# A linear-attention block with a gated feed-forward: the attention matrix M made in three fp32r passes, its late operands loaded elsewhere, and the instruction order given as a list of due times

## The chip, the cores and the metric

The kernel runs on one core of a Trainium2 chip. A core has a matrix engine (TensorE, PE in the profile, with PEld for its weight loads), a vector engine (VectorE, DVE), an activation engine (ScalarE, ACT), a general engine (GpSimd, POOL) and a queue engine (SyncE, SP) that here issues every DMA. Matrix products land in PSUM, which has eight banks of 128 x 512 fp32; other tiles lie in SBUF, in 128 partitions. The metric is the device time of one execution in microseconds; lower is better.

## The reference, cut to what matters

```python
def _A_ref(x, wqkv, wo):                 # x: 1 x 2048 x 512, 32 heads of 16
    q, k, v = split(x @ wqkv)
    phi = lambda t: where(t > 0, t + 1, exp(t)) + 1e-6
    pq, pk = phi(q), phi(k)
    kv = einsum("bhsd,bhse->bhde", pk, v)
    z = einsum("bhsd->bhd", pk)
    num = einsum("bhqd,bhde->bhqe", pq, kv)
    den = einsum("bhqd,bhd->bhq", pq, z)[..., None] + 1e-6
    return merge_heads(num / den) @ wo

def _B_ref(x, w_gate, w_up, w_down):     # 512 -> 1792 -> 512
    return (gelu(x @ w_gate) * (x @ w_up)) @ w_down

xn = layernorm(x)
return x + _A_ref(xn, wqkv, wo) * silu(_B_ref(xn, w_gate, w_up, w_down))
```

## The kernel before, in words

**Arithmetic.** All large products run in fp32r, the matrix engine's reduced fp32, in three passes: an operand is split into a high part (an ACT copy that rounds to fp32r) and a low part (the subtraction of the high part, on DVE or now and then on POOL), and high x high, high x low and low x high are added up in PSUM (`split`, line 640; `Sum`, line 646; `three`, line 671). Products of weights with 256 or 512 columns are further cut by a Strassen scheme of seven products in place of eight (`PRODUCTS`, line 212). A few small products were left in fp32.

**Stages.** In the first 135 us or so the tokens are normalised and turned, k and q are made from them, phi is taken, and `gps` gathers the sum over tokens of phi(k) times the normalised x (line 956). So v is never made: `GT` (four tiles, copied from `gps` after line 1140) times the v weights gives the k-v sums `pkv` of all heads (line 1203), which a mask cuts to the heads' own blocks, `kv4` (line 1205). `zacc` gathers phi(k) itself on POOL; a product with a matrix of ones, `pz` (line 1148), adds it up over the partitions for the denominator. Then the attention matrix M = kv4 x wo is made in four products, `pm` (lines 1207 to 1214), split into high and low, and stored to HBM as `m_d`. The attention's output is later one product `S` of M with the scaled phi(q) features (`sps`, in `attn`, line 1463), for four chunks of 512 tokens in the order 2, 3, 0, 1.

The feed-forward runs in two passes over the same 14 weight tiles, seven pairs of gate and up (`ffn`, line 1398). The first pass (`p` = 1) handles chunks 2 and 3 while the weights are split and stored to HBM as `w_d`; the second (`p` = 0) handles chunks 0 and 1 with the weights loaded back. `F` products (`fprod`, PSUM names FX, FY, FZ) make gate and up, `E` products (`down_strassen`, names dX, dY, dZ) go down to `acc`. The S products of chunk 2 stand between the E products at the end of the first pass, those of chunk 3 at the end of the second, and those of chunks 0 and 1 after everything.

**Places.** SBUF is cut by hand into pools of numbered places: `xf` holds the x forms in a high and a low place; `wp` three weight places used in a ring and a fourth for sums; `rawp` three places (R0, R1, TMP) for raw gate and up weights, which only the first pass reads; `dp` a draw place and four that hold accumulators in a pass; `up` 36 places of 128 x 512. A new tile in a place waits for all work on the tile before it. `load_m` (line 1451) loads M's two halves of 1 MB into the weight ring: at the end of the second pass they take the places of the last but two and the last but one weight tile. The features of chunk 3, eight pieces of 256 KB (high and low, loaded as such), then go to the low x place, those of chunk 0 to the high one, and those of chunk 1 to the low one again.

**Order.** Every instruction is recorded by `do` (line 270) with an engine, a cost in us and its tiles. `order` (line 309) decides the order on all engines ahead of time, from a list of PE keys written out by hand (`pe_keys`) and a due time `late` for each operation. `forward` (line 440) plays the program through with the recorded costs: at each step an engine takes, among its ready operations, the one with the least `late`; PE may run ahead of its list by 6 us (`AHEAD`, line 262). Before, eight passes of `latest` and `forward` found the due times, and 216 draws (`KEPT`, line 19) then altered some of them, each by at most 4 us for chosen operations (`altered`, line 332). The engines run the result in that order on the chip; a wait that comes out longer than the planner thought holds its whole engine.

Around the change, the hand-written list has the z product after five F products of the first pass, the k-v sums after twelve, and the four M products three F products later. M product number 0 to 3 use PSUM banks 6, 7, 5 and 6.

Of the kernel before, what the change touches and what calls it, by code (L numbers as in the profile page):

```python
# [15 lines left out]
P = 128  # L16
EPS_LN = 1e-5
EPS = 1e-6
KEPT = [
    (55, 70, [720000004]),  # L20
    (115, 135, [720000005]),
    (200, 270, [720000009]),
    (500, 560, [720000027]),
    (-1, 12, [720000035]),
    (70, 85, [720000040]),
    (-1, 12, [720000043]),
    (25, 40, [720000085, 720000134]),
    (200, 270, [720000140]),
    (-1, 12, [720000144]),
    (200, 270, [720000152]),  # L30
    (340, 420, [720000172, 720000184]),
    (100, 115, [720000203]),
    (340, 420, [720000233]),
    (500, 560, [720000243]),
    (40, 55, [720000247]),
    (560, 605, [720000257]),
    (200, 270, [720000279]),
    (340, 420, [720000290]),
    (500, 560, [720000362]),
    (200, 270, [720000390]),  # L40
    (55, 70, [720000517]),
    (40, 55, [720000540]),
    (340, 420, [720000555]),
    (270, 340, [720000602, 720000649, 720000655]),
    (340, 420, [720000658]),
    (270, 340, [720000690]),
    (500, 560, [720000887]),
    (12, 25, [720000899]),
    (55, 70, [720000957]),
    (500, 560, [720000974]),  # L50
    (40, 55, [720001218]),
    (-1, 12, [720001311]),
    (25, 40, [720001456]),
    (115, 135, [720001543]),
    (40, 55, [720001818]),
    (25, 40, [720001887]),
    (85, 100, [720001895]),
    (135, 200, [720001949]),
    (340, 420, [720002052]),
    (500, 560, [720002094]),  # L60
    (115, 135, [720002310]),
    (100, 115, [720002326]),
    (500, 560, [720002367]),
    (135, 200, [720002396]),
    (40, 55, [720002422]),
    (270, 340, [720002472]),
    (200, 270, [720002488]),
    (55, 70, [720002565, 720002605]),
    (115, 135, [720002669]),
    (100, 115, [720002694]),  # L70
    (55, 70, [720002734]),
    (40, 55, [720002796]),
    (100, 115, [720002858]),
    (40, 55, [720002901]),
    (340, 420, [720002982]),
    (70, 85, [720003200]),
    (420, 500, [720003430]),
    (-1, 12, [720003440]),
    (40, 55, [720003709, 720003813]),
    (70, 85, [720003981]),  # L80
    (115, 135, [720004064]),
    (25, 40, [720004170]),
    (100, 115, [720004402]),
    (500, 560, [720004624, 720004745]),
    (420, 500, [720004920]),
    (340, 420, [720005018]),
    (420, 500, [720005191]),
    (500, 560, [720005291]),
    (340, 420, [720005364]),
    (270, 340, [720005386]),  # L90
    (500, 560, [720005573]),
    (270, 340, [720005617]),
    (500, 560, [720005700, 720005753, 720005812]),
    (70, 85, [720005857]),
    (100, 115, [720005876, 720006137]),
    (200, 270, [720006523]),
    (340, 420, [720006542]),
    (270, 340, [720006565]),
    (500, 560, [720006740]),
    (270, 340, [720006762]),  # L100
    (420, 500, [720006797]),
    (100, 115, [720006937]),
    (25, 40, [720007069]),
    (100, 115, [720007820]),
    (270, 340, [720007916]),
    (200, 270, [720007997]),
    (100, 115, [720008028]),
    (40, 55, [720008434]),
    (70, 85, [720008559]),
    (40, 55, [720008706]),  # L110
    (55, 70, [720008751]),
    (-1, 12, [720008785, 720010301]),
    (25, 40, [720011151]),
    (-1, 12, [720011236]),
    (500, 560, [720011560]),
    (340, 420, [720011716]),
    (270, 340, [720011832]),
    (55, 70, [720011869, 720011995]),
    (40, 55, [720012578, 720013114]),
    (135, 200, [720013435]),  # L120
    (12, 25, [720013929]),
    (270, 340, [720014337]),
    (70, 85, [720015269]),
    (340, 420, [720015275]),
    (12, 25, [720015459]),
    (340, 420, [720016007]),
    (55, 70, [720016730]),
    (100, 115, [720016972]),
    (40, 55, [720017118]),
    (420, 500, [720019299, 720019742]),  # L130
    (25, 40, [720023341]),
    (560, 605, [720025689]),
    (200, 270, [720026707, 720027204]),
    (500, 560, [720027907]),
    (200, 270, [720029093]),
    (270, 340, [720029251]),
    (200, 270, [720030011]),
    (135, 200, [720030869]),
    (500, 560, [720031562]),
    (25, 40, [720032237]),  # L140
    (70, 85, [720033404]),
    (500, 560, [720034357]),
    (70, 85, [720034379]),
    (55, 70, [720034598]),
    (135, 200, [720037606]),
    (70, 85, [720037790, 720038397]),
    (200, 270, [720038864, 720039585]),
    (270, 340, [720041466]),
    (340, 420, [720041524]),
    (270, 340, [720041782]),  # L150
    (340, 420, [720043687]),
    (270, 340, [720043952]),
    (500, 560, [720044378]),
# [1492 lines left out]
```

## Time and profile before

| | us |
|---|---|
| median of 3 runs | 602.98 |
| lowest, highest | 602.73, 603.38 |
| the profiled execution | 602.79 |
| its span, first to last instruction | 601.1 |
| PE busy in the span | 593.4 |
| DVE busy | 499.3 |
| ACT busy | 367.4 |
| POOL busy | 242.0 |

The profile is one execution. Rows of the timeline give the start, the length, the engine, the line, the operation, the tile that is written, an arrow, the tiles that are read, and how many alike stand in a row; in square brackets stands how long the engine was idle before, and what released it. PE instructions overlap in the pipeline, so a single pass of 0.39 us in the rows occupies less than that of PE's time: the step from start to start is the measure. Nearly all products have the line of one helper (665), copies 632 and subtractions 638, so the tile names tell them apart. Rows "SPq" are the queue engine issuing DMAs.

### The profile page before, as it was taken

How to read it: one execution, taken by the hardware profiler on the slowest of the kernel's cores; microseconds unless marked ns; L12 is line 12 of the kernel's file. 1: busy time of each engine (PE TensorE's matmuls, PEld its weight loads, DVE VectorE, ACT ScalarE, POOL GpSimd, SP SyncE). 2: the span in 40 equal slices, each digit the busy share in tenths (PEclk: the TensorE clock that was granted, in tenths of full speed). 3: DMA queues.
4: the chain of work that ended last, by engine and by line, in shares of the span. 5: the costliest groups of instructions: out<-in, count | busy, mean ns of one | idle time of the engine just before them, and what ended most of it. 6: DMA issues, size and time to landing. Idle time of an engine off the chain costs nothing.

```text
span 601.1 us, 7826 instructions
## 1 busy us (share of the span) xinstructions
PE 593.4 (99%) x2626; PEld 481.2 (80%) x2626; DVE 499.3 (83%) x768; ACT 367.4 (61%) x663; POOL 242.0 (40%) x237
## 2 busy tenths in 40 slices
PE   8999999999999999999999999999999999999997
PEld 6887788777878888888887788888888888887786
DVE  6999988988788989999877675757698889898887
ACT  6687778877677765655545469567454544545620
POOL 4455856847636763605043730521122221206000
PEclk9999999999999999999999999999999999999999
DMA  7149977758986245467975899944656566648967
GB/s 271 46 131 281 287 229 237 235 186 275 379 314 226 91 158 209 158 210 299 336 231 184 323 393 381 332 163 140 210 174 210 175 228 201 218 156 269 364 219 269
DMA packets 78807, 141.27 MB, mean 235 GB/s; under 512 B 4656, under 2 KB 47664, under 8 KB 74672
## 3 DMA queue, kind: packets, MB, share of 16 engines
q1 hardware_dynamic: 78768, 140.79, 67.9%
q8 instruction: 20, 0.33, 0.2%
q14 instruction: 19, 0.16, 0.1%
HBM read 87.82 MB, written 52.95 MB: 234 GB/s over the span
## 4 chain that ended last, share of the span: by engine, by line
PE 85%; DVE 6%; DMA 6%; issue 1%; ACT 1%; SPq 0%; ACTq 0%; DVEq 0%
PE FX L665 25%; PE FZ L665 13%; PE dX L665 12%; PE FY L665 6%; PE gps L665 6%; PE dY L665 6%; PE X L665 4%; PE dZ L665 3%; DMA g<-g_d 2%; PE Z L665 2%; PE q L665 2%; PE sps L665 2%; PE k L665 2%; DMA pqh<-t_d 1%; PE Y L665 1%
## 5 line engine op out<-in xcount | busy, mean ns | idle before, releaser
L665 PE MATMUL FX<-Xh,w 128*128 128x512 f32 x448 | 134.7, 391 | 0.0
L1374 POOL TENSOR_TENSOR h<-h,g 128x512 f32<-128x512 f32 x28 | 38.9, 1390 | 150.5 <-DVE h L638 150.2
L665 PEld LDWEIGHTS FX<-Xh,w 128*128 128x128 f32 x448 | 83.9, 188 | 18.2 <-ACT fu L632 0.4
L665 PE MATMUL FX<-Xl,w 128*128 128x512 f32 x224 | 68.8, 389 | 0.0
L665 PE MATMUL FZ<-Xh,w 128*128 128x512 f32 x224 | 68.3, 391 | 0.0
L632 ACT COPY fu<-FX 128x512 f32<-128x512 f32 x56 | 32.9, 587 | 45.7 <-PE FX L665 43.2
L632 ACT COPY dY<-dX 128x512 f32<-128x512 f32 x56 | 32.0, 571 | 40.0 <-DVE acc L1328 30.6
L632 ACT CAST hfh<-sums 128x512 fp32r<-128x512 f32 x56 | 34.7, 622 | 27.9 <-DVE sums L638 27.7
L665 PEld LDWEIGHTS FZ<-Xh,w 128*128 128x128 f32 x224 | 42.0, 188 | 9.2 <-issue 0.5
L665 PEld LDWEIGHTS FX<-Xl,w 128*128 128x128 f32 x224 | 42.0, 188 | 8.8
L665 PE MATMUL dX<-hfh,dh 128*128 128x512 f32 x112 | 43.8, 395 | 0.3 <-ACT dY L632 0.3
L665 PE MATMUL dX<-hfl,dh 128*128 128x512 f32 x112 | 43.6, 391 | 0.0
L638 POOL TENSOR_TENSOR tmp<-raw 128x256 f32<-128x256 f32 x28 | 24.6, 886 | 47.2 <-ACT fu L632 24.1
L665 PE MATMUL dX<-hfh,dl 128*128 128x512 f32 x112 | 43.5, 390 | 0.0
L1328 DVE TENSOR_TENSOR acc<-acc,dX 128x512 f32<-128x512 f32 x48 | 32.9, 685 | 11.3 <-PE dX L665 10.7
L638 DVE TENSOR_TENSOR hfl<-sums,hfh 128x512 fp32r<-128x512 f32 x56 | 39.9, 721 | 2.5 <-ACT hfh L632 1.7
L1328 DVE TENSOR_TENSOR acc<-acc,dY 128x512 f32<-128x512 f32 x48 | 32.8, 684 | 10.8 <-PE dY L665 10.6
L638 POOL TENSOR_TENSOR sums<-draw 128x256 f32<-128x256 f32 x28 | 23.5, 850 | 34.9 <-DMA draw<-in_B_w_down 26.1
L638 DVE TENSOR_TENSOR hfl<-h,hfh 128x512 fp32r<-128x512 f32 x42 | 34.1, 817 | 1.6 <-ACT hfh L632 1.6
L638 DVE TENSOR_TENSOR h<-fu,FZ 128x512 f32<-128x512 f32 x28 | 19.2, 687 | 18.4 <-ACT fu L632 13.3
L665 PE MATMUL FY<-Xh,w 128*128 128x512 f32 x112 | 34.5, 390 | 0.0
L665 PE MATMUL FZ<-Xl,w 128*128 128x512 f32 x112 | 34.3, 389 | 0.0
(205 smaller groups left out, 1513.5 us busy)
## 6 DMA issues: line engine op xcount, KB each, us to landing
w<-w_d SPq DMA_DIRECT2D x17, 1792.0 KB, 7.9
w_d<-w SPq DMA_DIRECT2D x11, 1792.0 KB, 8.1
draw<-in_B_w_down SPq DMA_DIRECT2D x14, 512.0 KB, 6.4
w_d<-we SPq DMA_DIRECT2D x18, 256.0 KB, 2.1
x<-in_A_x SPq DMA_DIRECT2D x16, 256.0 KB, 4.5
q_d<-qp SPq DMA_DIRECT2D x16, 256.0 KB, 3.0
qz<-q_d SPq DMA_DIRECT2D x16, 256.0 KB, 3.7
q<-q_d SPq DMA_DIRECT2D x16, 256.0 KB, 3.9
```

Of the source, the lines that this page charges most:

```text
L632: do("ACT", act(n, src.psum), lambda o, i: nc.scalar.copy(o, i), dst, src, name=name)
L638: do(eng, c, lambda o, p, q: getattr(e, f"tensor_{op}")(o, p, q), dst, a, b, name=name)
L665: nc.tensor.matmul(o if r is None else o[:, r], a, b, start=first, stop=made == self.passes[r], skip_group_check=self.on or r is not None)
L1328: do("DVE", dve(D), lambda o, i: nc.vector.tensor_add(o, o, i), o, ps, name="acc")
L1374: do("POOL", pool(NC), lambda o, i: nc.gpsimd.tensor_mul(o, o, i), h, g, name="h")
```

## The change

1. The z product: `zacc` and the matrix of ones become fp32r tiles (ones by a copy, zacc by a split into two), and two fp32r passes replace the fp32 product.
2. M: `kv4` and the four wo tiles are split into high and low, and each M product becomes three fp32r passes. The wo pieces lie in the four `dp` places that the accumulators use later. In the hand-written list the M products come six F products after the k-v sums, not three.
3. At the end of the second pass M is loaded by a new function: its high half in two pieces to the raw places R0 and R1, its low half to one place of the weight ring. Chunk 3's features go to the next place of the weight ring (seven pieces) and to the raw place TMP (one). Chunk 0 then takes the low x place and chunk 1 the high one. The first pass's end still uses `load_m`.
4. The due times: `KEPT`, the draws and the passes of `latest` are gone; a list `LATE` of 3626 numbers in hundredths of a us, one for each operation in the order of recording, sets `late`, and one `forward` pass makes the order.

```diff
-KEPT = [
-    (55, 70, [720000004]),
...
-]
+LATE = [
+    -69366, -1060, -1881, 3921, -71310, -201580, -181669, -555, -187235, 1065, -80, 116, -316, 1915, 1687, 2067, 1147, 1663, -377, -1166, -3532,
...
+    58321, 58073, 58004, -53919, -56946, -43454,
 ]
...
-        best = None
-        done = self.ops_in_turn(pe)
-
-        for n in range(8):
-            self.latest(done, now, capacity=n > 0)
-            done = self.forward(pe)
-            end = max(t for t, _ in done)
-            if best is None or end < best[0]:
-                best = end, done, {o: o.late for o in self.ops}
-
-
-        for lo, hi, draws in KEPT:
-            for n in draws:
-                best = self.altered(n, lo, hi, pe, *best)
-        return [o for _, o in best[1]]
...
+        for o, late in zip(self.ops, LATE, strict=True):
+            o.late, o.lat0 = late / 100, o.lat
+        return [o for _, o in self.forward(pe)]
...
     pz = bank(7, "pz")
-    do("PE", 0.9, lambda o, a, b: nc.tensor.matmul(o, a, b, start=True, stop=True), pz, ones, zacc, key="z")
+    ones_r = tile_in("sm", "onr", [P, P], F32R, "ones_r")
+    do("ACT", 0.2, lambda o, i: nc.scalar.copy(o, i), ones_r, ones, name="ones")
+    zs = [tile_in("up", n, [P, D], F32R, f"z{n}") for n in (29, 32)]
+    split(*zs, zacc, D, "z")
+
+    def run_z(o, a, *zs):
+        for n, z in enumerate(zs):
+            nc.tensor.matmul(o, a, z, start=n == 0, stop=n == 1)
+    do("PE", 2 * PASS, run_z, pz, ones_r, *zs, key="z")
...
+    kvs = [tile_in("up", n, [P, KT, P], F32R, f"kv{n}") for n in (23, 33)]
+    split(*kvs, kv4, D, "kv")
+    wos = []
+    for g in range(KT):
+        v = tile_in("dp", 1 + g, [P, 2, D], F32R, f"wos{g}", 2)
+        wos.append([v.part(v.res[hl:hl + 1], (slice(None), hl)) for hl in range(2)])
+        split(*wos[g], wo_sb[g], D, "wo")
     for g in range(KT):
         pm = bank([6, 7, 5, 6][g], f"pm{g}")
-        do("PE", 0.9, lambda o, a, b, g=g: nc.tensor.matmul(o, a[:, g, :], b, start=True, stop=True),
-           pm, kv4, wo_sb[g], key=("m", g))
+        Sum(pm).add(("m", g), *three([[v[:, g] for v in kvs]], [wos[g]]), name="m")
...
+    def load_m_early():
+
+        high = [tile_in("rawp", r, [P, 2, D], F32R, f"Mh{r}") for r in (R0, R1)]
+        for r, m in enumerate(high):
+            src = View([m_d(k, ()).res[0] for k in (2 * r, 2 * r + 1)], m_d(0, (0, slice(None), slice(2 * r, 2 * r + 2))).get)
+            dma(m.map(lambda ap: ap.bitcast(F32)), src, 512)
+        low = tile_in("wp", ring("w", [0, 1, 2]), [P, KT, D], F32R, "Ml")
+        src = View([m_d(KT + k, ()).res[0] for k in range(KT)], m_d(KT, 1).get)
+        dma(low.map(lambda ap: ap.bitcast(F32)), src, 1024)
+        return [lambda k, rows: high[k // 2][:, k % 2, rows], lambda k, rows: low[:, k, rows]]
...
-    pe_keys += keys[2:5] + ["z"] + keys[5:KV] + [("kv", g) for g in range(KT)] + keys[KV:KV + 3]
-    pe_keys += [("m", g) for g in range(KT)] + keys[KV + 3:]
+    pe_keys += keys[2:5] + ["z"] + keys[5:KV] + [("kv", g) for g in range(KT)] + keys[KV:KV + 6]
+    pe_keys += [("m", g) for g in range(KT)] + keys[KV + 6:]
...
-    M = load_m()
+    M = load_m_early()
+    pq = [tile_in("wp", ring("w", [0, 1, 2]), [P, 7, D], F32R, "pqw", 7), tile_in("rawp", TMP, [P, 2, D], F32R, "pqt", 1)]
     vs = {hl: tile_in("xf", hl, [P, 14, NC], F32R, f"pq{hl}", 14) for hl in "lh"}
...
-    for c, hl in zip(CHUNKS[1:], "lhl"):
+    attn(CHUNKS[1], M, lambda i, n: pq[(i - KT) // 7].part(
+        pq[(i - KT) // 7].res[(i - KT) % 7:(i - KT) % 7 + 1], (slice(None), slice((i - KT) % 7, (i - KT) % 7 + 1))))
+    for c, hl in zip(CHUNKS[2:], "lh"):
         attn(c, M, lambda i, n, v=vs[hl]: v.part(v.res[i:i + n], (slice(None), slice(i, i + n))))
```

More of the change, by code (lines that the diff above doesn't have):

```diff
@@ L1 @@
-import random
 from contextlib import ExitStack
@@ L1506, in attn @@
             ps = bank(ring("sps", [3, 4, 2, 0, 1]), f"sps{c}{n}")
-            Sum(ps).add(("S", c, n), *three([[m[:, k, rows] for m in M] for k in range(KT)], forms_), name="S")
+            Sum(ps).add(("S", c, n), *three([[m(k, rows) for m in M] for k in range(KT)], forms_), name="S")
             if c == CHUNKS[0]:
```

273 lines of the change are left out of this document (2 added, 271 removed), and 177 rows, old and new, of the table LATE.

## The prediction

> **What bounds the kernel now.** I read the page first (busy shares, the granted clock, the chain that ended last), then the table of busy time by stage, then the order of time around each place that the change touches.
>
> ```profile
> span 601.1 us, 7826 instructions
> PE 593.4 (99%) x2626; PEld 481.2 (80%) x2626; DVE 499.3 (83%) x768; ACT 367.4 (61%) x663; POOL 242.0 (40%) x237
> PEclk9999999999999999999999999999999999999999
> PE 85%; DVE 6%; DMA 6%; issue 1%; ACT 1%; SPq 0%; ACTq 0%; DVEq 0%
> ```
>
> PE is busy 99% of the span, the clock is never cut, and the chain is PE for 85%. So the time is the matmuls' sum plus the places where PE stands. The stages (columns: busy time and count of PE, PEld, DVE, ACT, POOL, then clock, DMA share, GB/s) say where those are:
>
> ```profile
> 30.00:60.00 30.00, 29.70 (x134) 23.39 (x133) 27.62 (x45) 23.58 (x43) 17.04 (x18) 1.00 0.70 206
> 60.00:90.00 30.00, 29.48 (x135) 23.24 (x134) 27.21 (x49) 23.21 (x43) 21.56 (x21) 1.00 0.85 259
> 90.00:120.00 30.00, 29.94 (x130) 23.65 (x128) 26.49 (x38) 24.86 (x48) 21.53 (x20) 1.00 0.75 235
> 135.00:180.00 45.00, 45.00 (x205) 35.65 (x204) 35.45 (x49) 31.64 (x60) 26.53 (x28) 1.00 0.90 325
> 180.00:240.00 60.00, 60.00 (x266) 49.35 (x265) 53.62 (x82) 40.91 (x76) 34.27 (x31) 1.00 0.48 171
> 330.00:360.00 30.00, 29.71 (x128) 23.35 (x128) 20.41 (x30) 17.35 (x30) 17.21 (x15) 1.00 0.92 357
> 400.00:535.00 135.00, 135.00 (x597) 111.75 (x596) 111.90 (x167) 70.67 (x129) 28.53 (x27) 1.00 0.56 193
> 550.00:565.00 15.00, 14.28 (x59) 10.18 (x58) 13.38 (x20) 10.45 (x19) 5.98 (x5) 1.00 1.00 349
> 580.00:601.00 21.00, 17.02 (x87) 14.36 (x85) 17.76 (x31) 1.23 (x2) 0.00 (x0) 1.00 0.69 246
> ```
>
> From 400 to 535 us PE never stands: 135.00 / 597 = 0.226 us for one 512-column fp32r pass. That is my unit. PE stands 0.30 + 0.52 + 0.06 us between 30 and 120, 0.29 after 330, 0.72 after 550; the 3.98 after 580 are the last tile's multiply, add and store. A stop costs more than the idle shown, since the records overlap and the first pass after it is slow:
>
> ```profile
> 57.02 0.61 PE L665 MATMUL Z<-kq,Xh 128*128 128x512 f32 x2
> 57.84 1.20 PE L665 MATMUL Y<-kq,Xh 128*128 128x512 f32 x4 [0.21 <-ACT Y L632]
> 58.87 0.62 PE L665 MATMUL X<-kq,Xh 128*128 128x512 f32 x2
> ```
>
> Six passes take 58.87 - 57.02 = 1.85 instead of 1.36: 0.49 lost for 0.21 shown, a factor 2.3. The change touches three things of this bound: the number of PE slots, the stop after 550, and, by the new list, the order of everything.
>
> **Part 1, M and z in fp32r passes: PE has 1.15 us less.**
>
> ```profile
> 147.62 1.02 PE L1149 MATMUL pz<-zacc,blk 128*128 128x512 f32 x2
> 148.95 0.62 PE L665 MATMUL FX<-Xl,w 128*128 128x512 f32 x2
> 165.91 3.43 PE pm L1210 x8
> L1210 PE MATMUL pm<-wvo,kv 128*128 128x512 f32 x8 | 3.6, 592 | 0.0
> ```
>
> The z product starts at 147.62; two FX passes lie between it and 148.95, so it takes 1.33 - 2 x 0.226 = 0.88. It becomes two passes, 0.45: -0.43. The four fp32 M products (eight records) hold the chain for 3.43; twelve passes take 12 x 0.226 = 2.71: -0.72. Together -1.15, all on the path, since PE stands nowhere from 135 to 180.
>
> One sentence by a page: the Trainium skill, FP8 and Floating Point Precision, section TensorE Precision Notes, counts four passes for a true FP32 product; by it the five products would cost 5 x 0.904 = 4.52, the saving be 1.36, and the sum 0.2 lower. The rows (0.86 and 0.88 a product, 3.8 slots) do not quite bear that out and are taken.
>
> **What part 1 adds elsewhere: 0.** New are splits (one ACT cast, one DVE subtraction each) of z, of the masked k-v sums and of four wo tiles, and a cast of ones: six subtractions, seven casts. POOL and SP get nothing. The nearest rows:
>
> ```profile
> L638 DVE TENSOR_TENSOR dl<-sums,dh 128x512 fp32r<-128x512 f32 x24 | 16.5, 688 | 0.0
> L638 DVE TENSOR_TENSOR w<-tmp,w 128x512 fp32r<-128x512 f32 x10 | 9.5, 954 | 1.8 <-ACT w L632 1.8
> L632 ACT CAST dh<-sums 128x512 fp32r<-128x512 f32 x28 | 17.4, 620 | 3.3 <-POOL sums L638 2.4 <-PE dY L665 0.7 <-PE dZ L665 0.2
> ```
>
> DVE: 6 x 0.69 to 6 x 0.95 = 4.1 to 5.7 us; ACT: at most 7 x 0.62 = 4.3. Their cover is PE's own work from 135 to 180, where DVE is idle for 9.55 and ACT for 13.4. With them DVE is 88 to 91% busy there; 180 to 240 has 89% and PE stands for nothing. So 0, with 5.7 as the other end if the cover fails. A gain is excluded: nothing is taken from DVE or ACT.
>
> Are the inputs there in time?
>
> ```profile
> 138.22 1.30 POOL L945 TENSOR_TENSOR zacc<-zacc,kp 128x512 f32<-128x512 f32 x1 [0.63 <-DVE kp L934]
> 161.85 0.69 DVE L1206 TENSOR_TENSOR kv<-pkv,blk 128x512 f32<-128x512 f32 x1 [1.61 <-PE pkv L1203]
> 181.63 0.59 ACT L632 COPY acc<-dY 128x512 f32<-128x512 f32 x1 [1.82 <-PE dY L665]
> L628 SPq DMA_DIRECT2D wvo<-in_A_wo x4: 328/332/333, 115.8 to 142.8; - x4
> ```
>
> The last sum into zacc ends at 139.5; its split takes 1.3, and z runs at 147. M moves behind three more F products (18 passes, 4.1 us), to about 169.4 to 172.1; the masked sums exist at 162.5 and need 1.3 more. The wo pieces, issued by 142.8, borrow the accumulators' places until M is done; the first accumulator is written at 181.6, 9 us later. Nothing to pay.
>
> **Part 2, M and the third chunk's features load early in the second pass: -1.2 us.**
>
> ```profile
> 526.64 0.33 SPq L628 DMA_DIRECT2D M<-m_d  x1
> 540.70 0.33 SPq L628 DMA_DIRECT2D M<-m_d  x1
> 547.51 1.81 SPq L628 DMA_DIRECT2D pql<-t_d  x4
> 549.36 2.35 SPq L628 DMA_DIRECT2D pql<-tl_d  x4
> 546.85 0.62 PE L665 MATMUL FX<-Xl,w 128*128 128x512 f32 x2
> 553.47 1.20 PE L665 MATMUL sps<-pql,M 128*128 128x512 f32 x4
> 556.24 0.73 PE L665 MATMUL sps<-pql,M 128*128 128x512 f32 x2
> 557.67 0.73 PE L665 MATMUL sps<-pql,M 128*128 128x512 f32 x2 [0.70 <-DMA pql<-tl_d]
> 558.24 0.39 PE L665 MATMUL dZ<-hfl,dh 128*128 128x512 f32 x1
> ```
>
> The eight feature loads go where the low x forms lie; the last F pass that reads those starts at 546.85, and the loads are issued from 547.51. The S products start at 553.47 and catch up with them: four passes from 556.24 take 2.00 instead of 0.90 (1.10 lost), and one more slot before them was late by 0.1. After the change, M's high halves lie in the raw places, idle in the second pass, M's low half takes the weight slot free at 526.64, and seven of the eight pieces take the slot free at 540.70 (the eighth lies in a raw place). So these loads can start 6.8 us sooner, and the 1 MB of M no longer travels at 540.70. No bytes are added; SP gets one issue more (0.33). They needed 557.67 - 547.51 = 10.2 us from the first issue to the end of that stop; with as much again the last piece is there at 550.9, before S asks. Ends: 0 (another piece is late instead) and -1.7 (0.72 idle x 2.3, all of that stage's stop). I take -1.2, the row of the stop itself. Late next are the third chunk's output loads on SP; they feed DVE, not PE. The features of the last two chunks then go to one x place each, where before one place served twice; the S products of 576 on stood for nothing as it was.
>
> **Part 3, the new order: -0.7, and +0.2 at the start.** KEPT's 216 draws, applied to what eight passes of the planner gave, are replaced by 3626 stated due times, read by the same forward pass with the same durations. Nothing here is shown by a row; bounds: all other stops gone is (0.30 + 0.52 + 0.06 + 0.29) x 2.3 = -2.7; the other end is a stage as leaky as 60 to 90 (0.52 x 2.3 = 1.2 in 30 us) in the 180 us after 150, +7.2. Single entries of the list lie 2000 us before the start, where one draw of the old search moved an entry by 4 us at most: the list has been through far more such moves. They served the planner's time and not the chip's, so I credit a quarter of the gain, -0.7. By the list's first entries the loads at the start go x, x, wk, wk, x, wk, x, wk.
>
> ```profile
> 1.71 1.37 SPq L628 DMA_DIRECT2D wk<-in_A_wqkv  x3
> 3.13 0.43 SPq L628 DMA_DIRECT2D x<-in_A_x  x1
> 3.60 4.91 DMA wk<-in_A_wqkv
> 8.41 2.55 POOL L638 TENSOR_TENSOR kq<-wk,kq 128x512 fp32r<-128x512 f32 x2 [1.65 <-ACT kq L632]
> ```
>
> The fourth wk piece, on the chain before, is issued one load later (0.47). POOL is busy until 10.96 with its two subtractions anyway, which hides part of it: +0.2, ends 0 and +0.5.
>
> **Sum.** The profiled execution took 602.79 with 601.1 of span; it stands 0.19 below the median of 602.98. The terms add to -1.15 - 1.2 - 0.7 + 0.2 = -2.85: 599.94 for that execution, 600.1 against the median.
>
> **Rivals.** First, the early loads change nothing: the stop after 550 stays under another name (the same 2 MB still travel while the DMA share is 1.00, and s, g and x tiles are queued with them) and the order closes nothing. Then only part 1 and the start count: 602.98 - 1.15 + 0.2 = 602.0. For it speaks the full DMA share; against it the 6.8 us. Second, the order closes all other stops: 2.7 in place of 0.7, so 600.1 - 2.0 = 598.1. For it: the stops are of 0.2 us each, the kind that a reordering removes. Third, on the other side, DVE becomes late between 135 and 180. PE would stand for the w, h and kv pieces behind the six subtractions; DVE's idle 9.55 lies in scattered bits between dependent steps, and where none can be used the whole 4.1 to 5.7 goes on the path: 604.2 to 605.8. It decides from 4 us on. Against it stands the 89% of 180 to 240. A rule speaks for it: the Trainium skill, GPSIMD Engine Reference, section Key points, says that GpSimd shares its SBUF interfaces with VectorE and contends with instructions of two SBUF inputs, which all six are. The trace agrees in size: 0.95 for such a subtraction where POOL is busy, 0.69 where it seldom is. Fourth, also slower: the order opens stops after 150 at the rate of 60 to 90, +7.2 for the -0.7: 608.0; from half of that on it is slower than before. Against it: the unchanged forward pass left almost none there.
>
> **How the numbers follow.** Forecast 0.54 (599.0 to 601.3, each unknown within its nearer end), first rival 0.12, second 0.16, third 0.09, fourth 0.09. About 0.2% (1.2 us) can be told from no change here: the forecast and the second rival are faster, 0.70; the first is the same, 0.12; the last two slower, 0.18. Those two are left out of the range: 597.5 to 603.0.
>
> **What would show it.** Part 1: no fp32 pm or pz group, twelve pm passes in 2.7 us with F passes on both sides and no idle PE from 135 to 185. Part 2: feature loads issued near 540, S without a DMA wait, PE full from 550 to 565. Part 3: PE's idle time from 30 to 400 below 1.2, and the first k passes no later than 0.5. Wrong would be: DVE named as what PE waits for between 135 and 330, or a DMA named after 545.

## The result, and the profile after

The changed kernel takes 601.93 us in median (601.06 to 603.84, 22 runs) against 602.72 for the kernel before on the same chips (601.78 to 604.25, 22 runs): a ratio of 0.9982, 95% interval 0.9976 to 0.9987. That is 0.8 us faster: the interval excludes a ratio of 1, but the gain is less than the 1.2 us (0.2%) that the prediction set as the least to be told from no change, and little more than a quarter of the forecast 2.85.

The profiled execution took 602.27 with a span of 600.1. The page: span, busy time by engine, the chain by engine.

```profile
span 600.1 us, 7901 instructions
PE 593.2 (99%) x2630; PEld 481.0 (80%) x2630; DVE 505.1 (84%) x774; ACT 375.6 (63%) x672; POOL 251.6 (42%) x237
PEclk9999999999999999999999999999999999999999
PE 86%; DMA 8%; DVE 3%; ACT 1%; SPq 1%; issue 1%; ACTq 0%; DVEq 0%
```

PE is as busy as before, and the shares do not show where the time went. The table by stretch does, if one reads the number of matmuls in brackets and not the busy time. First the kernel before:

```profile
60.00:140.00 80.00, 79.42 (x347) 62.43 (x346) 70.59 (x107) 63.91 (x118) 54.35 (x50) 1.00 0.76 234
140.00:330.00 190.00, 190.00 (x846) 155.70 (x844) 163.07 (x247) 116.59 (x219) 88.64 (x89) 1.00 0.66 236
330.00:400.00 70.00, 69.66 (x302) 55.87 (x302) 46.88 (x66) 47.63 (x78) 28.90 (x25) 1.00 0.88 333
540.00:580.00 40.00, 39.28 (x168) 30.66 (x168) 32.64 (x50) 21.92 (x38) 11.26 (x10) 1.00 0.89 298
```

and the same stretches of the changed kernel:

```profile
60.00:140.00 80.00, 79.81 (x354) 63.63 (x353) 72.66 (x108) 65.73 (x122) 58.29 (x52) 1.00 0.79 242
140.00:330.00 190.00, 189.93 (x847) 155.36 (x846) 170.91 (x251) 118.08 (x221) 92.33 (x89) 1.00 0.66 235
330.00:400.00 70.00, 69.48 (x298) 54.44 (x297) 44.59 (x66) 49.42 (x78) 27.84 (x25) 1.00 0.90 340
540.00:580.00 40.00, 39.72 (x172) 31.60 (x171) 33.61 (x53) 21.21 (x37) 11.73 (x10) 1.00 0.76 251
```

Between 60 and 140 there are 7 matmuls more in the same time, between 540 and 580 4 more, between 330 and 400 4 fewer. Between 140 and 330 there is one more, but before, ten of the 846 were halves of fp32 products that take about 0.43 us each, 9 slots of 0.226 in excess of ten; the new 847 should have been 855. So 8 slots, 1.8 us, are missing there, and PE's idle time in that row is 0.07. What takes them looks like this in PE's timeline of the changed kernel:

```profile
174.31 0.39 PE L552 MATMUL dZ<-hfh,dh 128*128 128x512 f32 x1
174.73 0.73 PE L552 MATMUL FY<-Xh,w 128*128 128x512 f32 x2
175.30 0.62 PE L552 MATMUL FY<-Xl,w 128*128 128x512 f32 x2
```

From the dZ pass to FY go 0.42 us instead of 0.226, and the two FY passes take 0.57 instead of 0.45: 0.31 lost, with nothing in brackets, since the long records hide a gap of that size. I therefore added up, over all successive matmuls, the step from start to start less the steady step of that kind (0.226 for 512 columns), and call it lost time. It was worked out from the traces for every kernel here, in us:

| kernel | median, ratio to before [95%] | to 60 | 60–140 | 140–330 | 330–400 | 400 on |
|---|---|---|---|---|---|---|
| before | 602.72 | 10.05 | 4.37 | 0.53 | 1.89 | 2.31 |
| after | 601.93, 0.9982 [0.9976, 0.9987] | 9.99 | 2.84 | 2.19 | 2.91 | 1.30 |
| e1 M's high half late | 601.39, 0.9975 [0.9965, 0.9985] | 10.04 | 2.57 | 2.58 | 2.32 | 0.95 |
| e2 no low subtractions | 601.83, 0.9981 [0.9972, 0.9990] | 10.61 | 2.37 | 2.40 | 2.38 | 1.15 |
| e3 fp32 products | 602.72, 0.9998 [0.9990, 1.0007] | 9.89 | 2.46 | 2.22 | 2.42 | 0.99 |
| e9_pq_late | 608.69, 1.0095 [1.0082, 1.0108] | 10.07 | 3.08 | 2.83 | 2.43 | 7.27 |
| e4 old order, both parts | 603.74, 1.0017 [1.0006, 1.0028] | 9.82 | 4.14 | 3.21 | 1.93 | 1.57 |
| e5 old order, part 1 | 604.92, 1.0035 [1.0022, 1.0048] | 10.24 | 4.67 | 3.19 | 1.91 | 2.37 |
| e6 old order, part 2 | 601.99, 0.9987 [0.9978, 0.9997] | 9.90 | 4.24 | 0.63 | 1.67 | 1.75 |
| e7 new to 146, old behind | 608.08, 1.0083 [1.0066, 1.0101] | 10.32 | 2.55 | 10.12 | 1.89 | 2.48 |
| e8 part 1 in the gaps | 604.27, 1.0025 [1.0016, 1.0035] | 10.31 | 4.90 | 2.15 | 1.93 | 2.69 |
| e9_parts_in_gaps | 603.67, 1.0012 [1.0003, 1.0021] | 10.34 | 4.70 | 2.19 | 1.89 | 2.48 |
| e10 new to 175, old behind | 602.29, 0.9992 [0.9982, 1.0002] | 10.13 | 2.64 | 3.13 | 1.73 | 2.29 |
| e11 e10, mended | 600.61, 0.9963 [0.9951, 0.9975] | 10.03 | 2.52 | 2.83 | 1.60 | 1.22 |
| e12 gaps, mended | 601.64, 0.9983 [0.9974, 0.9991] | 10.28 | 4.22 | 1.93 | 1.93 | 1.28 |
| e13 new to 269 | 600.90, 0.9974 [0.9964, 0.9984] | 9.68 | 2.60 | 2.86 | 1.58 | 1.20 |
| e14 new to 320 | 601.61, 0.9981 [0.9972, 0.9990] | 10.35 | 2.80 | 3.14 | 1.85 | 1.16 |

(Lost time is that of one profiled execution. The level of the first two columns also rests on the step that is taken for the few 128-column products, which is the same for all kernels: read the differences between rows. The chips' medians of the kernel before lie between 602.53 and 602.97, so ratios are compared and not medians.)

The two spans differ by 0.95. PE's passes are 1.13 less (the sum of the steady steps, 576.59 and 575.46). The table gives -1.59 up to 140, +1.66 up to 330, +1.02 up to 400, -1.01 behind; with the passes that is -1.05, the tenth that is over lies at the ends. So the passes of part 1 and the loads of part 2 brought about what was forecast for them, 1.6 were gained in front, and 2.7 were lost between 140 and 400.

Part 1 in the timeline: two z passes, and the last of the twelve pm passes between F passes.

```profile
147.39 0.62 PE L1043 MATMUL pz<-z,ones_r 128*128 128x512 f32 x2
166.46 1.42 PE L552 MATMUL pm<-wos,kv 128*128 128x512 f32 x5
168.64 1.07 PE L552 MATMUL pm<-wos,kv 128*128 128x512 f32 x4
```

Part 2, SP's and PE's timeline: the features are issued from 538.87 on, 8.6 us before their place in the old order, and S runs through. No DMA is among PE's waits any more; the longest of them, the start left out, stand in the last two rows.

```profile
538.87 0.33 SPq L515 DMA_DIRECT2D pqw<-t_d  x1
539.72 1.37 SPq L515 DMA_DIRECT2D pqw<-t_d  x3
541.14 1.24 SPq L515 DMA_DIRECT2D pqw<-tl_d  x2
550.62 1.76 PE L552 MATMUL sps<-pqw,Mh 128*128 128x512 f32 x7
PE dX L552 <- ACT dY L519: 0.7, 2, 0.4
PE FY L552 <- ACT FY L519: 0.2, 1, 0.2
```

S starts at 550.62, 2.85 us sooner than before: the new order also asks sooner.

### The profile page after: what moved, and what is told of

The parts are those of the page before. It is cut to its first block, busy times and chain, and to the rows that moved or that the text cites. A ratio compares the mean times of both kernels' runs of the same rounds, so it can differ in the third digit from the quotient of the medians.

```text
span 600.1 us, 7901 instructions
## 1 busy us (share of the span) xinstructions
PE 593.2 (99%) x2630; PEld 481.0 (80%) x2630; DVE 505.1 (84%) x774; ACT 375.6 (63%) x672; POOL 251.6 (42%) x237
## 4 chain that ended last, share of the span: by engine, by line
PE 86%; DMA 8%; DVE 3%; ACT 1%; SPq 1%; issue 1%; ACTq 0%; DVEq 0%
PE FX L552 25%; PE FZ L552 13%; PE dX L552 11%; PE gps L552 6%; PE FY L552 6%; PE dY L552 6%; PE X L552 5%; PE sps L552 3%; PE dZ L552 3%; DMA Xh<-xh_d 2%; PE Z L552 2%; DMA Xl<-xl_d 2%; PE k L552 2%; PE q L552 2%; DMA pql<-t_d 2%; PE Y L552 1%
## 5 line engine op out<-in xcount | busy, mean ns | idle before, releaser
L552 PE MATMUL FX<-Xh,w 128*128 128x512 f32 x448 | 131.9, 391 | 0.1
L1275 POOL TENSOR_TENSOR h<-h,g 128x512 f32<-128x512 f32 x28 | 41.5, 1484 | 109.3 <-DVE h L525 109.2
L525 POOL TENSOR_TENSOR sums<-draw 128x256 f32<-128x256 f32 x28 | 25.0, 901 | 63.4 <-DMA draw<-in_B_w_down 37.5
L525 POOL TENSOR_TENSOR tmp<-raw 128x256 f32<-128x256 f32 x28 | 26.1, 943 | 54.2 <-DVE w L525 23.8
L525 DVE TENSOR_TENSOR hfl<-h,hfh 128x512 fp32r<-128x512 f32 x42 | 36.0, 858 | 4.4 <-ACT hfh L519 4.4
L519 ACT CAST hfh<-h 128x512 fp32r<-128x512 f32 x42 | 26.0, 622 | 17.3 <-DVE h L525 10.0
```

The lines of the kernel that those rows point to most:

```text
L519: do("ACT", act(n, src.psum), lambda o, i: nc.scalar.copy(o, i), dst, src, name=name)
L525: do(eng, c, lambda o, p, q: getattr(e, f"tensor_{op}")(o, p, q), dst, a, b, name=name)
L552: nc.tensor.matmul(o if r is None else o[:, r], a, b, start=first, stop=made == self.passes[r], skip_group_check=self.on or r is not None)
L1275: do("POOL", pool(NC), lambda o, i: nc.gpsimd.tensor_mul(o, o, i), h, g, name="h")
```

## The experiments

### In the new order: one cause at a time

**e1, M's high half late.** In the changed kernel M's high half is loaded at 344, in the stretch that lost 1.0. Here those loads are held until 450 us of the plan (442.8 on the chip); all else keeps its order.

```diff
-        return [o for _, o in self.forward(pe)]
+        out = [o for _, o in self.forward(pe)]
+        at = next(n for n, o in enumerate(out) if o.end > 450.0 and o.name != "held")
+        held = [o for o in out if o.name == "held"]
+        return [o for o in out[:at] if o.name != "held"] + held + [o for o in out[at:] if o.name != "held"]
...
-            dma(m.map(lambda ap: ap.bitcast(F32)), src, 512)
+            dma(m.map(lambda ap: ap.bitcast(F32)), src, 512, "held")
```

> The changed kernel, every engine's order as it is, but the two loads of M's high half, issued at 344 us between the reloads of the x forms, wait in the queue engine's order until 450 us or so. Theory that M's early load crowds the reloads of x, and that PE's stops from 360 to 370 come from that: those stops go (about 0.9 us of the 2.9 lost from 330 to 400), and the time falls by 0.5 to 1.0 against the changed kernel. Theory that the stops there come from the order of the instructions alone: within 0.2 of it.

Measured: 601.39. The stretch of 330 to 400 loses 2.32 against 2.91 in the changed kernel, but e2, e3 and e9_pq_late, which load M's high half early, lose 2.38 to 2.43 there: the half us is that one execution, the load is not the cause, and the intervals of e1 and the changed kernel overlap.

**e2, no low subtractions.** The six subtractions of low halves (z, the k-v sums, four wo tiles) are left out, and the passes read the high half instead, so the low parts are missing from the output. The number of passes and the order stay.

```diff
     split(*zs, zacc, D, "z")
+    plan.ops[-1].fn = lambda: None
+    zs[1] = View(zs[1].res, zs[0].get, zs[1].gen)
...
```

> The changed kernel, same order, with the six new subtractions left out: the low halves of z, of the k-v sums and of wo are not made, and the passes read the high half in their place, so that PE does the same work (the result is a little off). Theory that the subtractions make VectorE late from 135 on (the third rival in small): PE's losses from 140 to 330, 2.2 us against 0.5 before, fall by 1 or more and the time with them. Theory that the order makes these stops: the time stays within 0.3 of the changed kernel, and the stops stand at the same matmuls.

Measured: 601.83, against 601.93. VectorE has 4.2 us less to do between 140 and 330 (first row e2; 170.91 in the changed kernel), and PE gets no more done there:

```profile
140.00:330.00 190.00, 189.93 (x845) 155.04 (x844) 166.69 (x246) 118.29 (x221) 90.95 (x89) 1.00 0.65 235
```

In the new order it is not the subtractions that PE waits for.

**e3, fp32 products.** As e2, but the products are the fp32 ones of before, at the new places. They read the tiles of the high halves, which are plain fp32 copies here: ScalarE still makes each of them, in the same place and at the same 0.62 us.

```diff
-        v = tile_in("dp", 1 + g, [P, 2, D], F32R, f"wos{g}", 2)
+        v = tile_in("dp", 1 + g, [P, 2, D], F32, f"wos{g}", 2)
...
+        plan.ops[-2].fn = plan.ops[-1].fn = lambda: None
+        plan.ops[-3].fn = lambda g=g, pm=pm: nc.tensor.matmul(pm(), kvs[0]()[:, g, :], wos[g][0](), start=True, stop=True)
...
```

> As the run without the six subtractions, but z and M are made by fp32 products again, at the place and in the order of the changed kernel. Against the run without the subtractions this is the PE slots alone: 1.15 us slower if the first step of the prediction is right (0.43 for z, 0.72 for M), 1.36 by the four-pass count; 0 if PE's slots there are hidden.

Measured: 602.72, 0.89 above e2 where 1.15 was expected; the profiled execution of e3, 601.90, was its fastest, so its trace is not compared with e2's by span. Part 1's saving in passes is real. And with neither subtractions nor three passes, the new order still loses 2.2 between 140 and 330. The stops of 0.1 to 0.3 at 174.73, 187.49, 216 and 272 in the changed kernel's trace stand at the same products in e2 and e3; only the one of 0.30 before the fourth M product (166.46) is gone in e3.

No run takes away the casts, which come to 0.6 us each on ScalarE, the last of them at 161. But the changed kernel's trace shows ScalarE ahead of the next stop, that at 174.73:

```profile
170.48 0.64 ACT L519 CAST hfh<-sums 128x512 fp32r<-128x512 f32 x1
173.15 0.57 ACT L519 COPY dY<-dX 128x512 f32<-128x512 f32 x1 [2.03 <-PE dX L552]
174.11 0.57 ACT L519 COPY FY<-FX 128x512 f32<-128x512 f32 x1 [0.39 <-PE FX L552]
```

It had stood idle for 2.03 us, so it was not behind with casts, and it waited for PE's FX product before it could make the copy that PE's FY then waited for. The two products follow each other too closely: from 174 on the stops belong to where the order puts its instructions.

**e9_pq_late.** The seven feature loads are held back behind two g tiles in SP's queue (548.68 on), all else in its order.

```diff
...
+        held = [o for o in out if o.name == "pq3" and o.end > 500.0]
+        out = [o for o in out if o not in held]
+        at = out.index(after) + 1
+        return out[:at] + held + out[at:]
```

> The changed kernel, same order on all engines, but the seven loads of the third chunk's features that were issued from 538.9 are issued behind the two g tiles at 546 to 548, near where they were before the change. If the early load is worth what the prediction says, the stop after 550 is back and the time rises by 1.2 us; if another limit stands right behind it, by less than 0.3.

Measured: 608.69, 6.8 above the changed kernel. PE's waits, and the S group:

```profile
PE sps L560 <- DMA pqw<-t_d: 4.3, 1, 4.3
555.60 3.58 PE L560 MATMUL sps<-pqw,Mh 128*128 128x512 f32 x7 [4.31 <-DMA pqw<-t_d]
```

In the changed kernel the last of the seven lands at 548.15, 2.5 us before S starts; here they land from 551.72 to 558.07, and the lost time from 400 on rises from 1.30 to 7.27. Both expectations (1.2 and below 0.3) were far too low: 1.2 was the stop of the old order, in which S came 2.9 us later.

### Each part without the new order

For e4 to e14 the list of due times is replaced by the order itself, a list of 3626 instruction numbers (3625 or 3605 with one part undone):

```diff
-LATE = [
...
-        for o, late in zip(self.ops, LATE, strict=True):
-            o.late, o.lat0 = late / 100, o.lat
-        return [o for _, o in self.forward(pe)]
+ORDER = [
...
+        return [self.ops[n] for n in ORDER]
```

In e4 to e6 `ORDER` is the kernel before's order, with the parts' new instructions put in. New casts and subtractions stand a few us before they are needed, the three passes of each M product where the fp32 product stood; e6 has part 2 alone, with M's high half at about 450.

> Parts 1 and 2 without part 3: the instructions of the changed kernel, written out in the order list of the kernel before. The three-pass products stand where the fp32 products stood, the casts and subtractions of the new halves just ahead of them, M's high half is loaded at about 450, its low half at 526 and the features of the last third where the second load of M stood. Theory (the products and the early loads each pay what the traces show, 1.15 and about 1.0, and the new order as a whole takes more than a us back after 140): 2.0 to 2.4 faster than the kernel before, 600.4 to 600.8, with the start stops of the kernel before between 60 and 140 still there, and the stops between 140 and 400 at about 2.4 in sum as before. Rival (the order costs nothing, the parts themselves are worth less together than each alone, or the new halves make DVE late for the features): within 0.4 of the changed kernel, 601.6 to 602.0, with more idle PE between 140 and 200 than before.

> Part 1 alone in the order list of the kernel before: the three-pass products with all their casts and subtractions, the loads of M and of the features as before. Theory: 1.0 to 1.3 faster than the kernel before (z 0.43 and the four products 0.72), stops elsewhere as before, the stop at 540 to 580 still there with 2.2. Rival (the subtractions on DVE reach the path once the order has no room planned for them): 0 to 0.6 faster, with new idle PE between 135 and 180.

> Part 2 alone in the order list of the kernel before: fp32 products, M's high half loaded at about 450, its low half at 526, the features of the last third where the second load of M stood (seven loads from 540). Theory: 0.9 to 1.3 faster than the kernel before, with no wait of S on a DMA at 550 to 560 and the idle PE between 540 and 580 down from 2.2 to about 1. Rival (in the old order S comes later than in the new one, so its loads had less to gain, and the drain of the last third takes it back): 0 to 0.5 faster.

Measured: part 2 alone is 0.85 faster (601.99), just short of the 0.9 to 1.3 of the theory, and S waits for no DMA. Part 1 alone is 2.1 **slower** (604.92), and both together 0.9 slower (603.74): for these two, theory and rival both expected a gain. The rows of e5, PE's waits first:

```profile
PE pm L523 <- DVE m L496: 1.1, 1, 1.1
PE FX L523 <- ACT fu L490: 0.6, 1, 0.6
```

and its timeline, POOL, DVE, ACT and PE:

```profile
161.38 1.72 POOL L1246 TENSOR_TENSOR h<-h,g 128x512 f32<-128x512 f32 x1
161.89 1.76 DVE L496 TENSOR_TENSOR wos<-wvo,wos 128x512 fp32r<-128x512 f32 x1
167.41 0.68 DVE L496 TENSOR_TENSOR h<-g,FX 128x512 f32<-128x512 f32 x1
168.12 0.62 ACT L490 CAST hfh<-h 128x512 fp32r<-128x512 f32 x1 [1.66 <-DVE h L496]
169.13 1.55 ACT L490 CAST m<-pm 128x512 fp32r<-128x512 f32 x3
170.49 0.96 PE L523 MATMUL pm<-wos,kv 128*128 128x512 f32 x3 [1.09 <-DVE m L496]
```

The subtractions (one of them 1.76 us long, beside one of POOL's) make VectorE late with h; ScalarE, which works in order, stands 1.66 us before the cast of h, with the drains of the first M products (the copies that empty their PSUM banks) behind it; the fourth M product needs the first one's bank, and PE stands 1.09. The other stop is a cast of a wo tile that stands ahead of the drain `fu`. Lost time of 140 to 330 goes from 0.53 to 3.19: 2.66 for 1.13 saved. (That the subtractions start this is read from the trace; the old order was not run without them.)

### Is it the place of the new instructions?

**e8, e9_parts_in_gaps, e12.** The new casts and subtractions go where ScalarE and VectorE were idle before, one F product (six passes) moves ahead of the M products and one ahead of the last of them, where the expectation, which counts pairs of passes, has two M products ahead of it (e8 has part 1, the other both parts). e12 moves a few instructions once more, off the drains that they were seen to hold back:

```diff
 DVE order (around 128 and 139 us)
-wos subtraction, pkl
+pkl, wos subtraction
 ACT order (around 126 us)
-wos cast, u, we, kr, kr, pkh
+u, we, kr, kr, pkh, wos cast
 ACT order (around 172 us)
-m, w, w, fu
+fu, m, w, w
 SP order (around 470 us)
-features to pqt, w, q
+w, q, features to pqt
```

> Part 1 alone in the order list of the kernel before, as the run with part 1 alone, but the casts and subtractions of the new halves stand where ScalarE and VectorE were idle in the trace of before (ahead of a wait of 0.6 us or more each), the sum's subtraction stands behind the next h, and three F products stand before, two of the four M products before the next three, so that the tiles of M are drained before the fourth product needs a bank. Theory (part 1 saves its 1.15 of passes, and the stops of 2.66 more that the plain insertion showed between 140 and 330 came from where the new instructions stood): 0.8 to 1.2 faster than the kernel before, 601.6 to 602.0, with the stops of 140 to 330 at 0.5 to 0.9. Rival (VectorE is short between 135 and 175 wherever they stand): 604 to 605 as the plain insertion, stops there of 2 to 3.

> Both parts in the order list of before, with the new instructions in the idle places as in the run with part 1 in the gaps, M's high half at about 450 and the features of the last third early. Theory: the sum of the two parts, 1.15 and 0.9 measured, 2.0 faster than the kernel before, 600.6 to 601.0, faster than the changed kernel by about 1. Rival: within 0.4 of the changed kernel.

> As the run with both parts in the idle places of the old order, with these moved: the drain of FX ahead of the cast of the fourth M product and of the casts of weights (PE stood 0.8 us for it at 173), two subtractions of the weight's low halves behind the key features that they held back (0.5 us at 141), and the same load as in the other run (0.8 us at 482). Theory: 2.0 to 2.5 faster than that run, 601.0 to 601.7, about 1.5 faster than the kernel before, with the stops of 140 to 330 at 0.9 to 1.3. Rival (VectorE is short of time between 125 and 175 in the old order, so the delay is only passed on): 602.8 to 604.

Measured: e8 604.27, as its rival had it, and e9_parts_in_gaps 603.67, slower than both its theory and its rival. Neither is better than put in plainly, within the intervals: 140 to 330 loses 1.0 less than there, but 60 to 140 loses 4.9 and 4.7 instead of the 4.4 of before, and the stops that are left stand at the next drains. e12 is at 601.64, 2.0 less than e9_parts_in_gaps and within the theory's time. By the table, 1.2 of the 2.0 lie behind 400, where the feature load had held back the weight loads, and 0.5 between 60 and 140: these two went as the theory had it. The drain at 172 did not. Between 140 and 330 e12 still loses 1.93 where 0.9 to 1.3 was expected: the lost time from 140 to 175 falls by 1.09, and that from 175 to 330 rises by 0.82. Most of the delay was passed on to the next drains, as the rival had it for that stretch. And e12 (0.9983) is not faster by a measurable amount than part 2 alone (0.9987). In this order part 1 pays for itself and no more.

### New order in front, old order behind

**e7, e10.** At 146 and at 175 us both orders have had the same matmuls; e7 and e10 take the new order up to there and the old one from there on.

> Both parts, with the new order up to 146 us (where both orders have had the same matmuls) and the old order behind it. Theory (the new order gains about 1.5 before 140 and loses about 2.5 between 140 and 400): 3 to 4 faster than the kernel before, 599.0 to 599.8, faster than both kernels and about 1.5 faster than the run with the old order throughout. Rival (the stops between 140 and 400 follow from what the new front leaves behind, not from the order there): no faster than the changed kernel, 601.4 to 602, with the stops of 140 to 400 at 4 to 5 in sum.

> Both parts, with the new order up to 175 us, where both orders have had the same matmuls again and the new order has made M and stored it, and the old order behind it; M's high half at about 450. Theory (the new order gains about 1.5 up to 140, covers part 1, and its loss of 1.3 to 1.5 lies in its stops from 175 to 330 and of 0.5 to 1.0 between 330 and 400): 2.8 to 3.6 faster than the kernel before, 599.2 to 600.0, faster than both kernels; stops of 140 to 330 at 1.0 or less, of 330 to 400 at 1.9 or less. Rival (the late stops are what the new front leaves behind, in whatever order): 601.4 to 602.0, with 140 to 330 at about 2.2 again.

e7, 608.08, is a miss of my own making. The fourth wo tile is loaded late in the new order and its cast stands early in the old one:

```profile
153.78 0.62 ACT L490 CAST wos<-wvo 128x512 fp32r<-128x512 f32 x1 [6.15 <-DMA wvo<-in_A_wo]
PE FY L523 <- ACT FY L490: 6.4, 1, 6.4
```

One cast that waits for a DMA held every drain behind it. e10, 602.29, above the ranges of its theory and its rival too, has a smaller one of the same kind, two casts ahead of the drain `fu`: its waits and ACT's timeline at the seam.

```profile
PE FX L523 <- ACT fu L490: 1.8, 1, 1.8
174.57 1.14 ACT L490 CAST w<-tmp 128x512 fp32r<-128x512 f32 x2
175.61 0.59 ACT L490 COPY fu<-FX 128x512 f32<-128x512 f32 x1
```

**e11.** As e10, with three instructions moved:

```diff
 ACT order (around 175 us)
-FY, w, w, fu, hfh
+FY, fu, w, w, hfh
 SP order (around 470 us)
-features to pqt, w, q
+w, q, features to pqt
```

> As the run with the new order up to 175 and the old one behind, with three instructions moved: two casts of weights on ScalarE stand behind the next two drains (in that run they held back the drain of FX, and PE stood 1.8 us at 174), and the load of the third chunk's transposed features stands behind two loads of the old order (in that run it held them back, and PE stood 0.8 us at 482). Theory (each stop between 140 and 560 comes from one instruction that stands ahead of a drain, and goes with it): 2.5 to 3.2 us faster than that run in its stops, 599.2 to 600.2, with the stops of 140 to 330 at 1.0 to 1.4 and of 400 to 540 below 0.2; faster than both kernels. Rival (a stop taken away comes back at the next drain, since VectorE and ScalarE have fallen behind): 601.5 to 602.5, stops of 140 to 540 still above 3.5 in sum.

Measured: 600.61, 1.7 less than e10 and 2.25 less than the kernel before on its chip; its interval ends at 0.9975, just below the 0.9976 at which that of the changed kernel begins. It has the lowest ratio of all that ran, with e1 and e13 not to be told from it. (The two casts came to stand behind one drain and not behind two.) Its time is above the 599.2 to 600.2 of the theory and below the rival's 601.5: the stop at 482 went, and with it 1.1 of lost time behind 400, but 140 to 330 still loses 2.83 where 1.0 to 1.4 was expected. Of the 0.96 gained there up to 175, 0.68 comes back by 330. Two stretches of it:

```profile
140.00:330.00 190.00, 188.82 (x844) 155.11 (x843) 166.67 (x250) 117.56 (x221) 88.92 (x87) 1.00 0.64 234
330.00:400.00 70.00, 69.68 (x303) 56.19 (x302) 47.18 (x66) 47.27 (x78) 29.06 (x25) 1.00 0.89 336
```

303 matmuls from 330 to 400, as many as before with one to spare, and 5 more than the changed kernel. At the seam 0.8 of wait for `fu` is left (1.04 of lost time), and 0.66 of lost time at a subtraction behind it.

**e13, e14.** The seam at 269 and at 320, where both orders have had the same matmuls and differ in a few other instructions.

> Both parts; the new order up to 269 us, where both orders have had the same matmuls and but three other instructions are on different sides, and the old order behind it, with M's high half at about 450 and the features' load behind two loads of the old order. Theory (the seam at 175 cost the earlier run about 1.5 of stops since the two orders' drains were at different places there; the new order up to 269 has about 1.2 of stops after 140): 0.8 to 1.6 faster than the run with its seam at 175, 599.0 to 599.8, with the stops of 140 to 330 at 1.2 to 1.8 and of 330 to 400 at 1.6 to 1.9. Rival (a seam anywhere costs a stop of one to two us): 600.5 to 601.5.

> As the run with its seam at 269, with the seam at 320. Theory (the loss of the new order lies between 320 and 400): 599.2 to 600.2, within 0.4 of the run with its seam at 269, stops of 140 to 330 at about 2.0, of 330 to 400 at 1.6 to 1.9. Rival (the old order's stretch of 330 to 400 needs the old order ahead of it): stops of 330 to 400 at 2.3 or more, 600.8 to 601.5.

Measured: 600.90 and 601.61, both above the theory's ranges: the rival of e13 (a seam costs one to two us wherever it is) came nearest. At the seam e13 has stops of 0.48 and 0.45, e14 of 0.66 and 0.56; up to 260 the new order loses 1.3 behind 140. With the old order from 330 to 400 the loss there is 1.58 and 1.85, as the theory had it, so the changed kernel's extra there (0.4 to 1.0) lies in the order of that stretch.

## Why the prediction was right or wrong

The time, 601.93, lies in the stated range, but outside the forecast's own 599.0 to 601.3 and at the first rival's 602.0. It is not there by that rival's mechanism: that rival had the early loads change nothing and the order close nothing, and both did. Neither of the two signs that were named for being wrong showed up: no DMA holds PE after 545, and VectorE is not named between 135 and 330 in the list of PE's waits.

- **Part 1's passes (-1.15):** right. -1.13 in PE's steady steps; 0.89 between e3 and e2 in medians. The 1.36 that followed from the four passes of a true FP32 product, by the Trainium skill, FP8 and Floating Point Precision, section TensorE Precision Notes, is further off.
- **What part 1 adds elsewhere (0):** the size came out, for another reason than the one given, so by luck. In the changed kernel the subtractions are free (e2), and the only stop at part 1's own products is one of 0.30 (166.46, behind VectorE's subtraction for an earlier M product; its idle time of 0.03 is too short for the list of waits). But the step argued with VectorE's idle 9.55 us between 135 and 180 in the *old* profile, and in the old order the additions cost 2.66 (e5). All kernels with three passes, in whatever order, lose 1.9 to 3.2 between 140 and 330 (e7 and its 6.4 us wait apart); the two with fp32 products in the old order lose 0.53 and 0.63. In the old order that is 1.4 or more against 1.13 saved. The share of busy time said nothing of it; the third rival had the mechanism (idle time in scattered bits between dependent steps) and got 0.09.
- **Part 2 (-1.2):** right. -1.0 in the trace (4 slots more between 540 and 580), -0.85 alone (e6), no wait on a DMA. That S would ask at 553.5 as before was wrong; it asked at 550.6, and the loads issued from 538.87 on had landed by 548.15.
- **Part 3 (-0.7):** this step failed, by its sign. In the five kernels with the new order throughout, 1.3 to 2.0 are gained between 60 and 140, and 2.2 to 2.8 lost from 140 to 400. In the changed kernel's trace that is -1.53 and +2.68, in sum +1.15 in place of -0.7, and these 1.85 are nearly all of the 1.9 by which its span (0.95 shorter) misses the forecast; in e1, e2 and e3 it is +0.2 to +0.7. The medians say the same: e3, which has the new order and part 2 but neither the three passes nor the subtractions, is at 0.9998 of the kernel before, although part 2 alone is worth 0.85; an estimate from these two puts the order at +0.7. Second and fourth rival each came true in one half. The bound of the gain, idle time shown times 2.3, was wrong as well, since it left out what no idle shows: lost time from 30 to 400 was 8.76 us in the kernel before by the count of the table, not 2.7. The first check that was named for it (PE idle below 1.2 from 30 to 400) even came out right, 0.18 + 0.19 + 0.07 + 0.52 = 0.96 with 29.82 busy between 30 and 60, while the lost time of 30 to 400 rose from 8.76 to 10.25. The Trainium skill, Perfetto Trace Analysis, section Identifying the Most-Contended Engine, warns of just this: busy time of the matmuls says little since they are pipelined, and the busy share of the weight loads is the better measure. The rows of 330 to 400 agree: PE 69.66 before and 69.48 after, PEld 55.87 and 54.44.
- **Start (+0.2):** not seen. Up to 60 the lost time is 9.99 against 10.05.

So the sum fell short by the term of the order, which was credited with closing stops and opened others. The new instructions of part 1 do not make most of these: e3, without the subtractions and the three passes, keeps them, and ScalarE had worked off its casts before the stop at 174.73. From 330 to 400 the old order behind the new front (e11, e13, e14) takes 0.4 to 1.0 away, so there the order of the stretch itself is at fault. Why the new order leaves its stops between 140 and 330, and whether they are the price of making room for part 1, stays open; so does whether an order exists that has three passes and loses only 0.5 there. None of those tried did.

## What to carry to other kernels

In a kernel whose PE is 99% busy, compare matmuls per stretch, or start-to-start steps, and not idle time: most of what the new order lost here stood in stops of 0.1 to 0.3 us that no idle bracket shows. An addition to engines that work in order is priced by which drain stands behind it and not by the share of busy time; put it into the list and look at what it delays, and after mending a stop look at the next drains, since in e11 and e12 over two thirds of what was gained up to 175 was lost again by 330. And two orders can be spliced where they have done the same matmuls: e11 kept the front of the new one and the 330 to 400 of the old one, and came out below both kernels (just below the changed one, on another chip), though the seams cost 0.9 to 1.7 us.

## What was not expected of the hardware

- After a stop of PE the next two passes take 0.57 instead of 0.45 (174.73 above); the same 0.11 stands behind nearly every stop of these traces. A stop of 0.2 costs 0.31.
- The same subtraction of a wo tile on VectorE took 0.68 to 0.71 us in the changed kernel and up to 1.76 in e5 (161.89 above), beside a POOL instruction of 1.72 (161.38). Of the 128x512 fp32r subtractions in e5's trace, none of the 146 that ran clear of POOL took over 0.70; the 99 beside it took up to 1.78. The contention of GpSimd with VectorE that the Trainium skill, GPSIMD Engine Reference, section Key points, states was in the third rival at 0.95; here it is 2.5 times the undisturbed length.
- A load of 256 KB of wo took 2.7 to 8.8 us from issue to landing within e7, with a median of 2.9; the longest was issued 1.4 us behind a store of 1792 KB. A cast that stands in an in-order queue right behind such a load has to reckon with the longest.
